# Attention and two MoE layers on one core: the final addition steps through its columns in another order

## The chip, the cores and the metric

The kernel runs on one core of a Trainium2 chip. The metric is the device time of one execution, in microseconds (us). An execution is one launch: all inputs come from HBM and the result goes back to HBM. TensorE (PE) does matrix products and writes them to the accumulation memory PSUM; VectorE (DVE), ScalarE (ACT) and GpSimd (POOL) work on SBUF, the first two also on PSUM; SyncE (SP) issues transfers. Each engine works through its own instructions in program order and waits for others by semaphores.

## The reference

```python
# q, k, v: (4 batches, 8 heads, 576 tokens, 64), float32
q_d = q.reshape(B, H, Sd, factor, D).mean(axis=3)        # factor 4, Sd = 144; k_d, v_d alike
out_d = sm_attn(q_d, k_d, v_d)                           # softmax attention over 144 pooled tokens
out_up = np.repeat(out_d, factor, axis=2)                # each pooled row serves four tokens
mask = np.abs(pos[:, None] - pos[None, :]) < factor      # local attention: 7 neighbours
...
return (out_up + out_local).astype(np.float32)
# x: the sum, as (2304 tokens, 512)
g = h * (1.0 / (1.0 + np.exp(-h)))                       # layer 1: x @ w_in, then @ w_out (d_ff 2048)
g = np.where(h > 0.0, h, alpha * (np.exp(np.minimum(h, 0.0)) - 1.0))   # layer 2, the same shapes
```

The line that matters here is `out_up + out_local`: token t gets the local output of its own and the pooled output of token group t // 4.

## The kernel before, in words

The attention is cut into 16 units: 4 batches by 4 pairs of heads (`attend(i, due)`). Channels lie on the 128 partitions (two heads of 64), tokens lie along the columns. A unit goes through these steps, each a `Job` with an engine, a modelled duration and its predecessors:

- rows of q and k are loaded and turned by TensorE (L742), copied out of PSUM by ScalarE or VectorE (L770, L775), and pooled by fours on VectorE (tile `qkD`); v is pooled by TensorE for the first batch (L815) and by VectorE or GpSimd for the others (tiles `natv` or `lent` to `vd`);
- the local scores (L879) and the pooled scores (L955) go through their softmax: on VectorE the mask, the maxima and sums (tile `small`), on ScalarE the exponentials (L930, L974), on GpSimd mostly the two passes that subtract the maximum or multiply by the inverse sum (tile `ring`);
- TensorE turns the results (L1002, L1025); they are copied to SBUF (L1010, L1036); TensorE forms the pooled output (L1049, 144 columns, copied at L1057 to the tile `own` or `spare`, which the code calls `haD`) and the local output (L1114, in two PSUM banks of 288 columns);
- the join (L1131) adds both: it reads the local output from a PSUM bank `b`, the pooled output from `haD`, and writes the sum to the activations x in SBUF: `xa` (tokens 0 to 1151), `xb` (1152 to 1535) or `tail` (1536 to 2303). The bank becomes free when its join is done.

A unit has three joins of 288 columns: one with 128 partitions and two with 64 (the second bank holds its two heads swapped). In the third batch the cut at token 1536 splits the two 64-partition ones into 96 and 192 columns. There are 56 joins in all, with 40 x 288 + 8 x 192 + 8 x 96 = 13,824 columns.

Behind the joins, x is split into an upper part (`xh`, ScalarE, L1186) and a rest (`xl`, GpSimd or VectorE) and multiplied with the weights of layer 1 on TensorE (L1247 and, after the activation, L1290). These products run between the attention's. From about 238 us on everything is products (L1999, L2102, L1939, L2104, L1941). TensorE's short products at L447 and L460 fill gaps in the first 60 us; they compute nothing that is used.

The order of the work is made by a list scheduler while the program is built: it takes jobs when they are ready by modelled clocks of the engines and puts them out, so each engine's order is fixed in the program. The model's cost of a join depends on its number of columns alone. All work of VectorE and GpSimd passes through a recording helper and therefore stands at line 35 in the profile; tiles tell it apart.

Two other reads of VectorE step through memory, and the prediction uses them. The decoding of weights takes every second 32-bit word of `ws`:

```python
return st.rearrange("p (n w) -> p n w", w=2)     # L511
nc.vector.scalar_tensor_tensor(out(), st[:, :, 0], 13, out(), op0=ALU.logical_shift_right, op1=ALU.bitwise_or)   # L533
```

and the pooling of v sums four rows that lie 64 words apart:

```python
vn = hv.tile[j].rearrange("p (a r d) -> p a d r", a=2, r=FAC)     # L838
```

Of the kernel before, what the change touches and what calls it, by code (L numbers as in the profile page):

```python
# [53 lines left out]
def attention_moe_moe2_kernel(ctx, tc, q, k, v, wi1, wo1, wi2, wo2, out):  # L54
# [5 lines left out]
    P = 128  # L60
    FAC = 4
# [55 lines left out]
    HALF = S // 2  # L117
# [43 lines left out]
    def x_cuts(t0, n):  # L161

        at = sorted({t0, t0 + n} | {a for a, _, _ in X_AT if t0 < a < t0 + n})
        return [(a, e - a) for a, e in zip(at, at[1:])]

    def x_cols(c, t0, n, p0=0, p1=P):
        a, e, x = next(x for x in X_AT if x[0] <= t0 < x[1])
        assert t0 + n <= e
        return x[p0:p1, c, t0 - a:t0 - a + n]
# [500 lines left out]
    def attend(i, due):  # L670

        b, pr = pairs[i]
# [11 lines left out]
        haT, haD = Hold(SAT0 if early else SAT), Hold(SAD0 if early else SAD)  # L684
# [46 lines left out]
        for n_, cells in enumerate(([(0, c) for c in range(NTB - 1)], [(1, c) for c in range(NTB - 1)], [(0, NTB - 1), (1, NTB - 1)])):  # L731
            bank = Hold(banks, "a")
# [19 lines left out]
            o = 0  # L752
            for which in range(2):
                n = TB * sum(w == which for w, _ in cells)
                if n:
                    c0, nc_ = min(c for w, c in cells if w == which), n // TB
# [102 lines left out]
        for part, (s0, s1, halves_, outs) in enumerate(parts):  # L859
# [137 lines left out]
            for g0, g1_ in groups:  # L997
                bank = Hold(banks, "a")
# [16 lines left out]
            for a0_, a1_ in ((0, 2), (2, 3)):  # L1015
                bank = Hold(banks, "a")
# [49 lines left out]
            if b < QUAD_FROM:  # L1066
                for t in outs:
                    bank = Hold(banks, "a")

                    def out_l(t=t, bank=bank):  # L1070
                        vw = hw.tile.rearrange("p (n d) -> p n d", d=D)
                        for w in range(t * NW // 2, (t + 1) * NW // 2):
                            n = a0[w + 1] - a0[w]
                            c0 = (w % 2) * WIN + a0[w] - q0[w]
                            o = a0[w] - t * HALF
                            for j in range(2):
                                nc.tensor.matmul(
                                    bank.tile[j * D:(j + 1) * D, o:o + n],
                                    vw[j * WIN:(j + 1) * WIN, w, :],
                                    aT()[j * WIN:(j + 1) * WIN, w // 2, c0:c0 + n],  # L1080
                                    start=True, stop=True,
                                )

                    def join(t=t, bank=bank):
                        g0 = b * S + t * HALF
                        u0 = t * HALF // FAC
                        nc.vector.tensor_tensor(
                            x_cols(pr, g0, HALF).rearrange("p (m r) -> p m r", r=FAC),
                            bank.tile[:, :HALF].rearrange("p (m r) -> p m r", r=FAC),
                            haD.tile[:, u0:u0 + HALF // FAC].rearrange("p (m o) -> p m o", o=1).to_broadcast([P, HALF // FAC, FAC]),  # L1090
                            op=ALU.add,
                        )

                    pj = Job("P", 0.6, out_l, [lw] + [flips[g] for g in sorted(flips) if t == 1 or g == 0], lat=0.2, takes=[bank], uses=[hw, haT], mode="q")
                    end_ = due[t] if isinstance(due, tuple) else due + 0.5 * t
                    final.append(Job("V", 0.47, join, [pj, ups] + (sum(first_users.values(), []) if b == 1 else second_users if b else []), due=end_, uses=[bank, haD]))
                    x_written[pr, 2 * b + t] = final[-1]
                    if early:
                        first_users[pr].append(final[-1])
                continue  # L1100
# [21 lines left out]
            for t, p0, p1 in ((0, 0, P), (1, 0, D), (1, D, P)):  # L1122
                bank = banko[t]
                g0 = b * S + t * HALF
                for c0, n0 in x_cuts(g0, HALF):
                    c1 = c0 + n0

                    def join(t=t, bank=bank, p0=p0, p1=p1, g0=g0, c0=c0, c1=c1):
                        i0 = (p0 + t * D) % P
                        u0, n_ = (c0 - b * S) // FAC, (c1 - c0) // FAC  # L1130
                        nc.vector.tensor_tensor(  # L1131
                            x_cols(pr, c0, c1 - c0, p0, p1).rearrange("p (m r) -> p m r", r=FAC),
                            bank.tile[i0:i0 + p1 - p0, c0 - g0:c1 - g0].rearrange("p (m r) -> p m r", r=FAC),
                            haD.tile[p0:p1, u0:u0 + n_].rearrange("p (m o) -> p m o", o=1).to_broadcast([p1 - p0, n_, FAC]),
                            op=ALU.add,
                        )

                    end_ = due[t] if isinstance(due, tuple) else due + 0.5 * t
                    job = Job(
                        "V", 0.16 + 0.00106 * (c1 - c0), join,  # L1140
                        [pj, ups] + (sum(first_users.values(), []) if b == 1 else second_users if b else []), due=end_, uses=[bank, haD],
                    )
                    if p0 or c0 > g0:
                        job.after([x_written[pr, 2 * b + t]])
                    final.append(job)
                    x_written[pr, 2 * b + t] = job
                    if early:
                        first_users[pr].append(job)
# [977 lines left out]
    with tc.manual_schedule():  # L2126
# [17 lines left out]
        for i in range(len(pairs)):  # L2144
            b_, pr = pairs[i]
# [110 lines left out]
```

## Time and profile before

| | |
|---|---|
| median of 3 runs | 852.47 us (851.71 to 852.82) |
| profiled execution, its own time | 852.25 us |
| its span, first to last instruction | 850.5 us |
| TensorE, busy | 842.7 us (99%) |
| VectorE, busy | 670.5 us (79%) |
| ScalarE, busy | 559.6 us (66%) |
| GpSimd, busy | 200.3 us (24%) |

Busy shares are averages over stages: up to about 217 us attention and layer 1 run beside each other and all engines take part; after it TensorE has products back to back. TensorE's busy time is modelled from pipelined products and also covers the filling products. The time of the profiled execution is 1.75 us longer than its span, for what lies around the instructions.

### The profile page before, as it was taken

Reading aid. Unit: us, or ns where it says so; the run is one execution under the profiler, and the core shown is the slowest. Engines: PE = TensorE matmul, PEld = TensorE weight load, DVE = VectorE, ACT = ScalarE, POOL = GpSimd, SP = SyncE. Lnnn points to the kernel's source line nnn. Section 1 sums busy time; section 2 is a strip of 40 time slices with the busy share of each in tenths; the row PEclk is TensorE's granted clock in tenths of the full one; section 3 lists DMA queues with packets and bytes.
Section 4 is the critical chain, followed back from the end, with each engine's and each line's share of the span. In section 5 each row is a group of like instructions: output and inputs, shape, how many; then the busy total and the mean of one; then the engine's idle time right before and its main releaser. Section 6 shows DMA issues by size and latency. Waiting matters only on the chain.

```text
span 850.5 us, 17258 instructions
## 1 busy us (share of the span) xinstructions
PE 842.7 (99%) x6507; PEld 780.8 (92%) x6507; DVE 670.5 (79%) x1348; ACT 559.6 (66%) x1270; POOL 200.3 (24%) x229
## 2 busy tenths in 40 slices
PE   8999999999999999999999999999999999999998
PEld 6778787778899999999999998899998999999998
DVE  6777776665889998958969789479889999487497
ACT  5778764455479886455398596377499884473672
POOL 7677785574200100000000121000020102002012
DMA  9888785331346354043287475163686670561612
GB/s 167 195 186 184 163 260 121 91 92 59 124 127 195 122 173 126 1 150 106 70 258 266 175 240 198 75 223 106 214 277 214 216 270 5 208 201 38 220 42 75
DMA packets 120483, 132.59 MB, mean 156 GB/s; under 512 B 65040, under 2 KB 97040, under 8 KB 120272
## 3 DMA queue, kind: packets, MB, share of 16 engines
q1 hardware_dynamic: 118032, 130.90, 50.7%
q8 instruction: 51, 0.84, 0.4%
q10 hardware_dynamic: 2368, 0.59, 0.4%
q14 instruction: 32, 0.26, 0.1%
HBM read 89.26 MB, written 42.21 MB: 155 GB/s over the span
## 4 chain that ended last, share of the span: by engine, by line
PE 96%; DVE 1%; POOL 1%; ACT 1%; DMA 0%; issue 0%; SPq 0%; POOLq 0%; ACTq 0%; DVEq 0%
PE b L1999 34%; PE b L1941 14%; PE b L2102 8%; PE b L1290 8%; PE b L2104 8%; PE b L1247 8%; PE b L1939 7%; PE b L742 2%; PE b L1114 1%; PE b L879 1%; PE b L1002 1%; PE b L1025 1%; PE b L1049 1%; PE b L955 1%; PE b L815 1%; PE b L447 0%
## 5 line engine op out<-in xcount | busy, mean ns | idle before, releaser
L1999 PE MATMUL b<-xhr,xaw 128*128 128x384 f32 x288 | 77.3, 335 | 0.0
L1290 PE MATMUL b<-gx,w 128*128 128x512 f32 x288 | 75.3, 399 | 0.0
L1999 PE MATMUL b<-xhr,w 128*128 128x384 f32 x256 | 66.8, 335 | 0.0
L1247 PE MATMUL b<-xh,w 128*128 128x512 f32 (+1 forms) x176 | 62.9, 394 | 1.0 <-POOL w L35 0.6
L1290 PEld LDWEIGHTS b<-gx,w 128*128 128x128 f32 x288 | 52.1, 188 | 11.0 <-issue 1.0
L2011 ACT COPY hg<-b 128x384 f32<-128x384 f32 x60 | 29.0, 483 | 45.5 <-PE b L1999 45.2
L35 DVE TENSOR_TENSOR part<-b,part 128x256 f32<-128x256 f32 (+3 forms) x94 | 43.1, 506 | 17.5 <-PE b L1941 16.1
L35 DVE TENSOR_TENSOR b<-b,hg 128x384 f32<-128x384 f32 x60 | 33.6, 561 | 27.9 <-PE b L1999 20.4
L35 POOL TENSOR_TENSOR ring<-ring,small 128x640 f32<-128x640 f32 (+1 forms) x41 | 47.7, 1170 | 29.5 <-DVE small L35 29.2
L1999 PE MATMUL b<-xlr,xaw 128*128 128x384 f32 x160 | 53.5, 334 | 0.0
L1999 PEld LDWEIGHTS b<-xhr,xaw 128*128 128x128 f32 x288 | 52.4, 188 | 0.0
L35 DVE TENSOR_TENSOR xlr<-tail,xhr 128x768 fp32r<-128x768 f32 x42 | 39.9, 954 | 14.3 <-ACT xhr L1416 13.9
L1941 PE MATMUL b<-w,gx 128*128 128x256 f32 x264 | 49.8, 283 | 0.0
L2102 PE MATMUL b<-grw,w 128*128 128x384 f32 x192 | 49.7, 334 | 0.0
L2102 PE MATMUL b<-gx,w 128*128 128x384 f32 x192 | 49.3, 334 | 0.0
L2104 PE MATMUL b<-w,gx 128*128 128x512 f32 x156 | 46.9, 389 | 0.0
L1999 PEld LDWEIGHTS b<-xhr,w 128*128 128x128 f32 x256 | 46.4, 188 | 0.2
L1999 PE MATMUL b<-xlr,w 128*128 128x384 f32 x128 | 42.8, 334 | 0.0
L35 POOL TENSOR_TENSOR gx<-hg,grw 128x384 fp32r<-128x384 f32 x4 | 4.4, 1108 | 160.5 <-ACT grw L1416 160.5
L1416 ACT CAST xhr<-tail 128x768 fp32r<-128x768 f32 x42 | 35.7, 850 | 9.4 <-DVE tail L35 9.3
L2104 PE MATMUL b<-w,grw 128*128 128x512 f32 x132 | 41.6, 389 | 0.0
L1247 PEld LDWEIGHTS b<-xh,w 128*128 128x128 f32 x176 | 32.4, 188 | 8.5 <-POOL w L35 1.0
(352 smaller groups left out, 2616.8 us busy)
## 6 DMA issues: line engine op xcount, KB each, us to landing
ws<-in_moe_w_in_dram SPq DMA_DIRECT2D x30, 512.0 KB
ws<-in_moe_w_out_dram SPq DMA_DIRECT2D x30, 512.0 KB
tailr<-xs SPq DMA_DIRECT2D x28, 384.0 KB
xs<-xhr SPq DMA_DIRECT2D x21, 384.0 KB
xs<-xlr SPq DMA_DIRECT2D x21, 384.0 KB
x<-part SPq DMA_DIRECT2D x6, 768.0 KB
tail<-x SPq DMA_DIRECT2D x12, 384.0 KB
vw<-in_v_dram SPq DMA_DIRECT2D x28, 144.0 KB
```

The source lines that it names most:

```text
L35: ins = x(*args, **rest)
L742: nc.tensor.transpose(bank.tile[:, n * TB:(n + 1) * TB], row(which, c)[:TB], ident[:TB, :TB])
L815: nc.tensor.matmul(bankv[j].tile[:HS, c * D:(c + 1) * D], pooler()[rows_, n, :], vw[rows_, w, :], start=n == 0, stop=n == len(POOLED_BY) - ...
L1247: nc.tensor.matmul(ph.tile[:, o:o + m_], w[a][:, c, :], x, start=c == 0 and m == 0, stop=c == KC - 1 and m == 2, skip_group_check=True,)
L1290: nc.tensor.matmul(y[d].tile[:, :W], wo[m // 2][:, d * P:(d + 1) * P], gg(m % 2, 0, W), start=f == 0 and m == 0, stop=fin and m == 2)
L1416: a = Job("A", ACT_[width], lambda: nc.scalar.copy(hi(), at()), preds, gate)
L1939: nc.tensor.matmul(y, wm[:, sl], gm, start=first, stop=last_, skip_group_check=True)
L1941: nc.tensor.matmul(y, gm[:, sl], wm, start=first, stop=last_, skip_group_check=True)
L1999: nc.tensor.matmul(acc_, a[:, cs], b[:, c, :], start=fresh and c == 0 and m == 0, stop=c == 1 and m == 2, skip_group_check=True,)
L2011: snap[after, j] = [Job("A", ACT_[NB], lambda dst=dst, acc_=acc_: nc.scalar.copy(dst, acc_), [], gate, due=soon)]
L2102: nc.tensor.matmul(y[d][:, :NB], wm[:, sl], gm, start=first, stop=last_)
L2104: nc.tensor.matmul(y[d], gm[:, sl], wm, start=first, stop=last_)
```

## The change

Only the form of the join's access patterns changes. Before, the walk over a join's columns was in the order in which they lie in memory: pooled column m outside, its four tokens r inside. Now r is outside and m inside: the walk reads columns 0, 4, 8, ... of the PSUM bank and writes them to columns 0, 4, 8, ... of x, then columns 1, 5, 9, ..., and so on. The pooled operand, which was read four times in place for each column, is now read through in order, four times over. The values added and the places written are the same.

```diff
                         nc.vector.tensor_tensor(
-                            x_cols(pr, c0, c1 - c0, p0, p1).rearrange("p (m r) -> p m r", r=FAC),
-                            bank.tile[i0:i0 + p1 - p0, c0 - g0:c1 - g0].rearrange("p (m r) -> p m r", r=FAC),
-                            haD.tile[p0:p1, u0:u0 + n_].rearrange("p (m o) -> p m o", o=1).to_broadcast([p1 - p0, n_, FAC]),
+                            x_cols(pr, c0, c1 - c0, p0, p1).rearrange("p (m r) -> p r m", r=FAC),
+                            bank.tile[i0:i0 + p1 - p0, c0 - g0:c1 - g0].rearrange("p (m r) -> p r m", r=FAC),
+                            haD.tile[p0:p1, u0:u0 + n_].rearrange("p (o m) -> p o m", o=1).to_broadcast([p1 - p0, FAC, n_]),
                             op=ALU.add,
                         )
```

The same edit stands in a second join (L1087) behind `if b < QUAD_FROM`; QUAD_FROM is 0, so that branch is not built. No instruction moves on any engine. On VectorE 56 rows change their shape. The first piece is VectorE's order in the first unit (at about 21 us of the profile); `b_98` and `b_99` are PSUM banks, `own` is the pooled output, `small` holds maxima and sums:

```order
 L35 COPY xa<-b_93 128x480
-L35 TENSOR_TENSOR xa<-b_98,own 128x288
-L35 TENSOR_REDUCE small<-small 128x3
-L35 RECIPROCAL small<-small 128x3
-L35 TENSOR_TENSOR xa<-b_99,own 64x288
+L35 TENSOR_TENSOR xa<-b_98,own 128x4x72
+L35 TENSOR_REDUCE small<-small 128x3
+L35 RECIPROCAL small<-small 128x3
+L35 TENSOR_TENSOR xa<-b_99,own 64x4x72
 L35 TENSOR_REDUCE small<-b_96 128x5
```

The two joins stand at the same places; a contiguous run of 288 columns has become 4 rows of 72. The second piece is VectorE's order in the first unit of the third batch (at about 127 us), where the joins stand between the steps of another unit's softmax:

```order
-L35 TENSOR_TENSOR xb<-b_94,own 128x288
-L35 TENSOR_TENSOR tail<-b_96,own 64x192
-L35 TENSOR_REDUCE small<-ring_118 128x10
-L35 TENSOR_REDUCE small<-small 128x10
-L35 RECIPROCAL small<-small 128x10
-L35 TENSOR_TENSOR xb<-b_96,own 64x96
+L35 TENSOR_TENSOR xb<-b_94,own 128x4x72
+L35 TENSOR_TENSOR tail<-b_96,own 64x4x48
+L35 TENSOR_REDUCE small<-ring_118 128x10
+L35 TENSOR_REDUCE small<-small 128x10
+L35 RECIPROCAL small<-small 128x10
+L35 TENSOR_TENSOR xb<-b_96,own 64x4x24
```

Here too only the shapes differ: the sums of `ring` and their inverse stay behind three joins.

## Rows read from the trace of the kernel before

**Rows 1.** The page's busy times: engine, busy us (share of the span), instructions.
```profile
PE 842.7 (99%) x6507; PEld 780.8 (92%) x6507; DVE 670.5 (79%) x1348; ACT 559.6 (66%) x1270; POOL 200.3 (24%) x229
```

**Rows 2.** The table of stretches: busy us of each engine, clock, DMA, GB/s.
```profile
21.30:34.20 12.90, 12.45 (x285) 9.74 (x277) 12.17 (x33) 8.94 (x29) 9.01 (x10) 1.00 0.92 248
...
58.00:126.00 68.00, 67.96 (x799) 54.95 (x798) 50.69 (x103) 49.03 (x127) 53.16 (x54) 1.00 0.82 197
126.00:217.00 91.00, 90.64 (x1032) 71.34 (x1029) 55.23 (x127) 46.17 (x134) 51.50 (x58) 1.00 0.34 88
217.00:850.50 633.50, 630.44 (x3817) 614.18 (x3815) 522.71 (x1016) 425.88 (x900) 54.23 (x49) 1.00 0.47 158
```

**Rows 3.** Groups on VectorE: output, inputs, shapes, count | busy us, mean ns | idle.
```profile
L35 DVE TENSOR_TENSOR xa<-b,own 64x288 f32<-64x288 f32 x12 | 5.5, 454 | 3.6 <-PE b L1114 3.2
...
L35 DVE TENSOR_TENSOR tail<-b,own 64x192 f32<-64x192 f32 x8 | 2.8, 352 | 0.2
...
L35 DVE TENSOR_TENSOR xb<-b,own 64x96 f32<-64x96 f32 x8 | 2.0, 255 | 5.2 <-PE b L1114 2.5 <-ACT own L1057 2.5
```

**Rows 4.** The same view: contiguous reads, and reads that step.
```profile
L35 DVE SCALAR_TENSOR_TENSOR raw<-ws,raw 128x512 int32<-128x512 int32 x48 | 33.1, 691 | 5.2 <-ACT raw L529 5.1
...
L35 DVE TENSOR_REDUCE qkD<-qk 128x144 f32<-128x576 f32 x20 | 14.0, 742 | 0.1
...
L35 DVE TENSOR_TENSOR part<-b,part 128x512 f32<-128x512 f32 x12 | 7.5, 682 | 7.9 <-PE b L1941 7.9
L35 DVE TENSOR_REDUCE vd<-natv 72x128 f32<-72x512 f32 x7 | 7.5, 1066 | 0.0
```

**Rows 5.** The chain that ended last, 18 to 60 us: start, us, what.
```profile
21.34 0.46 DVE xa L35
...
42.08 0.46 DVE xa L35
...
42.56 0.03 ACT xh L1186
...
42.88 0.26 ACT qk L770
```

**Rows 6.** Waits of TensorE's weight loads, 20 to 36 us: us, times, longest.
```profile
PEld b L815 <- DVE xa L35: 0.4, 1, 0.4
```

**Rows 7.** Timeline of VectorE, 38 to 43 us: start, us, what, idle before.
```profile
38.75 1.43 DVE L35 TENSOR_TENSOR xa<-b,own 64x288 f32<-64x288 f32 x3
41.10 1.43 DVE L35 TENSOR_TENSOR xa<-b,spare 64x288 f32<-64x288 f32 x3 [0.92 <-ACT xh L1186]
```

**Rows 8.** Timeline of all engines, 126 to 131 us.
```profile
126.85 0.73 DVE L35 TENSOR_TENSOR xb<-b,own 64x96 f32<-64x96 f32 x2
...
127.61 0.36 DVE L35 TENSOR_TENSOR tail<-b,own 64x192 f32<-64x192 f32 x1
...
129.30 2.13 POOL L35 TENSOR_TENSOR ring<-ring,small 128x640 f32<-128x640 f32 x2 [3.37 <-DVE small L35]
...
130.62 0.31 PEld L1002 LDWEIGHTS b<-own,ring 128*128 128x128 f32 x3 [0.43 <-POOL ring L35]
```

**Rows 9.** The chain that ended last, 128 to 143 us.
```profile
138.53 0.36 DVE tail L35
...
138.93 1.66 PE b L1247 x6
```

**Rows 10.** Timeline of all engines, 178 to 184 us.
```profile
178.35 1.43 DVE L35 TENSOR_TENSOR tail<-b,own 64x288 f32<-64x288 f32 x3
...
181.24 2.13 POOL L35 TENSOR_TENSOR ring<-ring,small 128x640 f32<-128x640 f32 x2 [1.59 <-DVE small L35]
...
183.41 0.40 PEld L1025 LDWEIGHTS b<-own,ring 112*72 112x72 f32 x4 [0.40 <-POOL ring L35]
```

**Rows 11.** Timeline of VectorE behind two other triples, at 72.86 and 163.36 us.
```profile
75.92 0.42 DVE L35 SCALAR_TENSOR_TENSOR t<-t,b 128x256 f32<-128x256 f32 x1 [0.91 <-ACT t L1269]
...
165.63 0.89 DVE L35 SCALAR_TENSOR_TENSOR ring<-b,mask 128x320 f32<-128x320 f32 x2 [0.60 <-PE b L879]
```

More of the change, by code (lines that the diff above doesn't have):

```diff
@@ L1087, in join @@
                         nc.vector.tensor_tensor(
-                            x_cols(pr, g0, HALF).rearrange("p (m r) -> p m r", r=FAC),
-                            bank.tile[:, :HALF].rearrange("p (m r) -> p m r", r=FAC),
-                            haD.tile[:, u0:u0 + HALF // FAC].rearrange("p (m o) -> p m o", o=1).to_broadcast([P, HALF // FAC, FAC]),
+                            x_cols(pr, g0, HALF).rearrange("p (m r) -> p r m", r=FAC),
+                            bank.tile[:, :HALF].rearrange("p (m r) -> p r m", r=FAC),
+                            haD.tile[:, u0:u0 + HALF // FAC].rearrange("p (o m) -> p o m", o=1).to_broadcast([P, FAC, HALF // FAC]),
                             op=ALU.add,
```

## The prediction, as it was put on record

> **What bounds the kernel now.** I read the page's busy times first. TensorE has 842.7 us of a span of 850.5 us; VectorE, where the change sits, has 670.5 us, or 79% [rows 1]. A longer VectorE operation costs time only where TensorE comes to wait for it. So I read the table of stretches next: from 217 us on TensorE is busy for 630.4 of 633.5 us and no join is left there, so the joins, which run from 21 to 217 us, decide by how much that last stretch starts later. Before it, VectorE is busy for 50.7 of 68 us and then 55.2 of 91 us, so it has gaps that can swallow something; but from 21.3 to 34.2 us it is busy for 12.17 of 12.90 us and has none to speak of [rows 2]. TensorE's clock column is 1.00 throughout, its full 2.4 GHz level, so no term comes from the clock. Then I followed each of the 16 units in the timeline, the chain and the list of waits: what follows its joins on VectorE, who waits for that, and how wide the next gap is.
>
> **The operation itself.** Nothing is added, removed or moved; 56 joins change the step of two of their three streams. Before, a join of 288 columns takes 454 ns and one of 96 takes 255 ns [rows 3]. That is (454 - 255) / 192 = 1.04 ns per column and 255 - 96 x 1.04 = 155 ns besides. A contiguous addition of 512 columns takes 682 ns [rows 4], which is 155 + 512 x 1.03. So the join already runs at the full rate, fourfold reading of the pooled column included, and there is nothing to gain per column.
>
> Now the read of PSUM and the write to SBUF both step by 4 words (16 bytes); only the pooled operand becomes contiguous. No row has a step of 4 words. Two rows bracket it. The decoding of weights reads every second word: 691 ns for 512 columns, 1.05 ns per column, no penalty. The pooling of v steps by 64 words: 1066 ns for 512, or (1066 - 155) / 512 = 1.78 ns per column, where the same reduction of contiguous columns takes (742 - 155) / 576 = 1.02 [rows 4]. So a stepping stream costs between nothing and 0.76 ns per column; two of them between nothing and 1.52, if their costs add. With 13,824 columns that is 0 to 21 us of VectorE.
>
> The row at 2 words is free and the row at 64 is not. The Trainium skill, page "SBUF — State Buffer", section "Door 1: The DMA port swizzle", has a note that SBUF is reached in lines of 16 bytes, that two accesses in a row must fall in one line for the full rate, and that PSUM has lines of 8 bytes. The free row agrees (two of its words lie in 16 bytes), and by this note a step of 16 bytes pays on both streams, which speaks against the change. The page "Vector Engine (DVE) Microarchitecture Reference", section "5.2 Measured stream behaviour on trn2 (trn3 not measured)", asks for runs of two adjacent words; by that the 2-word row would have to be slow, and its 691 ns says that it isn't.
>
> Between 0 and 1.52 I take 1.0 ns more per column: the free row still uses every second word that it passes, the join only every fourth, and it does so on two streams at once, so I put it nearer to the row that pays and a little over one stepping stream. A join of 288 then takes 454 + 288 = 742 ns, and VectorE has 13.8 us more.
>
> **Where it lies on the path.** Five places have no cover.
>
> 1. 21.3 to 34.2 us. Six joins stand in VectorE's row of work. The chain of waits runs through the first at 21.34 us [rows 5], and at its end TensorE's L815 waits for the bank of the sixth, with 0.4 us of waiting already [rows 6]. 6 x 288 ns = 1.73 us. Of the stretch's 0.73 us of idle time most is hand-over between neighbours; I let 0.3 us absorb: 1.43 us.
> 2. The fourth unit's three joins at 41.10 us [rows 7]. The chain goes through them: the split `xh` on ScalarE waits for the last (42.08 to 42.54), and behind it in ScalarE's order stands the copy of `qk` (42.88), which leads to the pooled scores [rows 5]. 864 columns: 0.86 us. The third unit's joins at 38.75 us cost nothing: behind them VectorE is idle for 0.92 us, waiting for others [rows 7].
> 3. 126.85 us. Three joins (96, 288 and 192 columns) stand ahead of the sums that GpSimd waits 3.37 us for, and the weights of TensorE's L1002 wait 0.43 us for GpSimd [rows 8]. 576 columns: 0.58 us. The other 288 columns of that unit lie behind those sums and are covered.
> 4. 136.3 to 138.9 us. The chain goes through five joins, the last at 138.53 us, and then to TensorE's L1247 at 138.93, which needs the bank [rows 9]. 864 columns: 0.86 us.
> 5. 178.35 us. Behind the three joins come sums; GpSimd is idle for 1.59 us until they are done, and TensorE's L1025 waits 0.40 us for GpSimd [rows 10]. 0.86 us.
>
> Together 1728 + 864 + 576 + 864 + 864 = 4896 columns of 13,824, or 4.90 us less 0.3 = 4.6 us.
>
> The other 8928 columns I cost at nothing. Their cover is VectorE's next gap: 0.91 us behind the joins at 72.86 us, 0.60 us behind those at 163.36 us, where another 0.26 us stays over [rows 11] and falls on sums that TensorE needs later. With the cover gone they would cost 8.9 us more. What each covered triple makes late is the next unit's mask and sums on VectorE, then GpSimd's passes over `ring`, then L1002 and L1025; TensorE has products of layer 1 to do meanwhile, and its order is fixed. Nothing brings time back: after 217 us TensorE runs without a break.
>
> **The sum.** 852.25 us (the profiled execution's own time, 1.75 us over its span; 0.22 under the median of the runs) + 4.6 = 856.85 us; I say 856.8. With one stepping stream's 0.76 ns it is 852.25 + 3.72 - 0.3 = 855.7. With 1.52 ns it is 852.25 + 7.44 - 0.3, and the joins of 288 grow by 438 ns, so three of them (1.31 us) overrun the gaps of 0.92, 0.91 and 0.60 us by 0.39, 0.40 and 0.71 us: 860.9.
>
> **Rivals.**
>
> - *The step is free* (the other side). If VectorE serves a step of 4 words like that of 2 words (691 ns), the joins stay at 454 ns and the time at 852.3 us. For it: the only small step in the trace costs nothing. Against it: the 64-word row, and that PSUM must be read in steps too, which no row shows. It decides below about 0.4 ns per column, where 4896 columns less 0.3 us fall under 1.7 us. 0.18.
> - *The two streams add.* Read and write each wait on their own and one after the other, so the price is 1.52 ns per column and the covers overrun: 860.9 us. For it: a join has no buffer that a row would show. Against it: a stream that steps alone costs 0.76, and read and write of one instruction can run side by side. 0.16. (The Trainium skill's Microarchitecture Reference, section 5.2, lists an output that steps 24 words at 2.50 ns per column; an estimate from that page, 1.46 more per column, would give about 860.5 us. No row here shows a stepping output.)
> - *Only the first 46 us count.* TensorE has 0.36 us of idle time from 126 to 217 us [rows 2], nearly all at place 4; places 3 and 5 show only waiting weight loads. It may have more in hand than I think; then places 1, 2 and 4 alone give 1.43 + 0.86 + 0.86: 855.4 us, and without place 4 854.5. For it: 0.4 us of waiting by a weight load is not yet TensorE idle. Against it: each load started right when GpSimd was done. 0.17.
>
> **How the numbers follow.** My forecast (prices of 0.76 to 1.25 ns and five places: 855.7 to 858.1 us) gets 0.43. The rest of 0.06 is for more than 861 us, where covers fail that I counted. A measurement of this kernel tells some 0.2%, or 1.7 us, from no change. Faster by that: 0.02, since no join can lose more than some ns. Within it: 0.18, of which 0.16 is the rest of the free step and 0.02 the low end of the third rival. Slower: 0.80, all the rest. The range goes from 852.3, the free step's time, to 861.0, the adding streams'; outside stay the 0.06 above and about half of the free step, 0.15 in all.
>
> **What would show it.** In the profile of the changed kernel: the group of joins 64x288 (now 4 x 72) at about 742 ns, between 454 and 892; VectorE's busy time at 684 us; TensorE's waits for `xa` at L815 and for `tail` at L1247 longer by about 0.3 and 0.9 us; the stretch of unbroken products after 217 us as long as before, but begun 4.6 us later, 2.3 us of it lost by 46 us and the rest between 126 and 184 us. I am wrong if the joins stay at 454 ns, or if they are slower and TensorE starts its last stretch on time; then the covers were wider than the gaps that I read.

## The result and the profile after

The changed kernel takes 856.92 us (median of 5 runs, 855.36 to 857.35) where the kernel before takes 852.36 us (5 runs, 851.48 to 852.82): a ratio of 1.0051, with an interval of 1.0036 to 1.0066. The change costs about 4.6 us; the forecast was 856.8. The profiled execution took 856.92 us, 4.67 us more than the one before (852.25); its span is 855.2 us, 4.7 more.

The page's busy times after (columns as in [rows 1]):

```profile
PE 843.7 (99%) x6507; PEld 780.6 (91%) x6507; DVE 680.3 (80%) x1348; ACT 560.0 (65%) x1270; POOL 203.3 (24%) x229
```

VectorE has 9.8 us more than before. The joins' groups on VectorE, which answer to [rows 3]:

```profile
L35 DVE TENSOR_TENSOR xa<-b,own 64x288 f32<-64x288 f32 x12 | 8.2, 680 | 3.6 <-PE b L1114 3.2
...
L35 DVE TENSOR_TENSOR tail<-b,own 64x192 f32<-64x192 f32 x8 | 4.0, 500 | 0.2
...
L35 DVE TENSOR_TENSOR xb<-b,own 64x96 f32<-64x96 f32 x8 | 2.7, 332 | 5.0 <-ACT own L1057 2.6 <-PE b L1114 2.3
```

A join of 288 columns has grown by 226 ns, or 226 / 288 = 0.785 ns per column; those of 192 and 96 by 148 and 77 ns, 0.77 and 0.80 per column. The cost is per column; the time besides stays about the same, (680 - 332) / 192 = 1.81 ns per column leaving 158 ns, before 155. The table of stretches after, by its own time (the last row begins 4.7 us later than that of [rows 2], as much as the span has grown):

```profile
21.30:34.20 12.90, 12.04 (x291) 9.68 (x280) 12.32 (x33) 8.37 (x26) 8.56 (x10) 1.00 1.09 260
58.00:126.00 68.00, 66.88 (x769) 53.25 (x768) 52.61 (x102) 48.50 (x127) 51.90 (x53) 1.00 0.80 192
126.00:217.00 91.00, 89.49 (x1004) 70.03 (x1001) 59.34 (x127) 45.57 (x133) 53.37 (x59) 1.00 0.36 95
...
221.70:855.20 633.50, 630.42 (x3817) 614.15 (x3815) 522.78 (x1017) 425.77 (x900) 57.17 (x49) 1.00 0.47 158
```

The last 633.5 us hold the same 3817 products with the same busy time (630.42 us, before 630.44): nothing is lost or given back there, and the clock column stays at 1.00. TensorE's idle time has grown in each of the three rows above that one: from 0.45 to 0.86 us between 21.3 and 34.2 us, from 0.04 to 1.12 between 58 and 126, and from 0.36 to 1.51 between 126 and 217. The forecast had nothing between 58 and 126 us.

What TensorE's products wait for in the whole span after (us, times, longest):

```profile
PE b L955 <- DVE qkD L35: 1.2, 1, 1.2
...
PE b L1247 <- DVE tail L35: 1.0, 1, 1.0
PE b L1025 <- DVE yo L35: 0.8, 1, 0.8
PE b L1002 <- POOL ring L35: 0.7, 3, 0.4
...
PE b L1247 <- DVE xa L35: 0.5, 1, 0.5
PE b L1247 <- DVE t L35: 0.4, 1, 0.4
```

Before, this list had 1.0 for `qkD`, 0.3 for `tail`, 0.4 for `yo` and 0.2 for GpSimd's `ring`, and neither the wait for `xa` nor that for `t` at L1247.

Since no instruction moves on any engine, each product of TensorE can be paired with the same one before, and the difference of the two start times shows where time is lost. The table gives how much the lag grows, in us, at the place where it grows (time of before; medians over the products between two places). "Start" is the difference already there behind the first loads, at about 14 us; it differs by over a microsecond from run to run and has nothing to do with joins. The other columns are runs of the next section: the stepping order in one batch of four only, and a copy ahead of each join of before.

| place, us | after | only batch 0 | only batch 1 | only batch 2 | only batch 3 | copy ahead |
|---|---|---|---|---|---|---|
| start | 0.17 | -0.07 | -1.27 | -1.00 | 0.02 | -1.30 |
| 24.5 (L1025) | 0.42 | 0.42 | 0.31* | 0.38* | 0.31* | 1.10* |
| 34 (L815) | 0.00 | 0.00 | 0.05 | 0.05 | 0.05 | 0.05 |
| 42.5 (L879) and 45.9 (L955) | 0.72 | 0.70 | 0.01 | 0.00 | 0.00 | 0.62 |
| 59.9 (L1247) | 0.50 | -0.02 | 0.46 | -0.02 | 0.02 | 0.33 |
| 68.6 (L1049) | 0.15 | 0.03 | 0.21 | 0.03 | 0.01 | 0.14 |
| 95.6 (L1247) | 0.39 | 0.00 | 0.39 | 0.03 | 0.02 | 0.27 |
| 119.6 (L1002) | 0.41 | 0.00 | 0.46 | 0.00 | 0.00 | 0.26 |
| 130.6 (L1002) | 0.36 | 0.00 | 0.01 | 0.35 | 0.00 | 0.45 |
| 138.9 (L1247) | 0.61 | -0.02 | 0.02 | 0.65 | -0.03 | 0.68 |
| 165.3 (L955) | 0.17 | 0.00 | 0.00 | 0.13 | 0.00 | 0.11 |
| 179.9 (L1247) and 183.4 (L1025) | 0.78 | 0.02 | 0.01 | 0.00 | 0.76 | 0.55 |
| all | 4.68 | 1.07 | 0.66 | 0.59 | 1.18 | 3.24 |

The fields with * hold a difference of 0.3 us or more at about 28 us (L815) that also comes up in a run whose joins are as short as before (0.27 us, the read in steps below), so in the runs of batches 1 to 3 it isn't the joins' doing. The 1.10 of the last column are 0.29 at 24.5 us and 0.81 at 28, more than in any other run; TensorE's load at L815 sits idle there for 0.7 us, and the profile names no releaser. What causes this is open.

### The profile page after: what moved, and what is told of

The parts are those of the page before. It is cut to its first block, busy times and chain, and to the rows that moved or that the text cites. A ratio compares the mean times of both kernels' runs of the same rounds, so it can differ in the third digit from the quotient of the medians.

```text
span 855.2 us, 17258 instructions
## 1 busy us (share of the span) xinstructions
PE 843.7 (99%) x6507; PEld 780.6 (91%) x6507; DVE 680.3 (80%) x1348; ACT 560.0 (65%) x1270; POOL 203.3 (24%) x229
## 4 chain that ended last, share of the span: by engine, by line
PE 90%; DVE 4%; POOL 2%; issue 1%; DMA 1%; ACT 1%; SPq 0%; POOLq 0%; ACTq 0%; DVEq 0%
PE b L1999 34%; PE b L1941 14%; PE b L2102 8%; PE b L2104 8%; PE b L1939 7%; PE b L1290 6%; PE b L1247 5%; POOL ring L35 1%; PE b L742 1%; PE b L1114 1%; PE b L1002 1%; DMA nat<-in_q_dram 1%; DVE small L35 1%; PE b L1049 1%; PE b L1025 1%
## 5 line engine op out<-in xcount | busy, mean ns | idle before, releaser
L1999 PE MATMUL b<-xhr,xaw 128*128 128x384 f32 x288 | 77.3, 335 | 0.0
L1999 PE MATMUL b<-xhr,w 128*128 128x384 f32 x256 | 66.9, 335 | 0.0
L1247 PE MATMUL b<-xh,w 128*128 128x512 f32 (+1 forms) x176 | 63.0, 395 | 2.5 <-DVE tail L35 1.0
L1999 PE MATMUL b<-xlr,xaw 128*128 128x384 f32 x160 | 53.5, 334 | 0.0
L1999 PEld LDWEIGHTS b<-xhr,xaw 128*128 128x128 f32 x288 | 52.4, 188 | 0.0
L1999 PEld LDWEIGHTS b<-xhr,w 128*128 128x128 f32 x256 | 46.4, 188 | 0.2
L1999 PE MATMUL b<-xlr,w 128*128 128x384 f32 x128 | 42.8, 334 | 0.0
L1247 PEld LDWEIGHTS b<-xh,w 128*128 128x128 f32 x176 | 32.4, 188 | 10.3 <-DVE tail L35 1.4
```

The lines of the kernel that those rows point to most:

```text
L1247: nc.tensor.matmul(ph.tile[:, o:o + m_], w[a][:, c, :], x, start=c == 0 and m == 0, stop=c == KC - 1 and m == 2, skip_group_check=True,)
L1999: nc.tensor.matmul(acc_, a[:, cs], b[:, c, :], start=fresh and c == 0 and m == 0, stop=c == 1 and m == 2, skip_group_check=True,)
```

## The experiments

Two questions were open. Which of the two stepping streams pays, and from which step on? And does VectorE's longer time alone explain the 4.6 us, at places that the forecast did not have? Edits are given against the changed kernel's join unless they say otherwise.

### Which stream pays

One stream at a time. First the bank is read in steps of 4 and x is written in order; then the other way round.

```diff
-  x_cols(...).rearrange("p (m r) -> p r m", r=FAC),           # first run: the write
+  x_cols(...).rearrange("p (r m) -> p r m", r=FAC),
-  bank.tile[...].rearrange("p (m r) -> p r m", r=FAC),        # second run: the read
+  bank.tile[...].rearrange("p (r m) -> p r m", r=FAC),
```

> The 56 joins read PSUM in steps of 4 words as in the change, but write x contiguously, so the tokens inside each join's columns land in another order (the output is not the reference's). The changed kernel's join of 64x288 took 680 ns, 0.78 ns per column over the 454 ns of before. Theory A (a stream that steps sets the rate, and two that step run side by side): about 680 ns here too, TensorE's first L1999 about 4.5 us later than before. Theory B (both streams pay, and the prices add): about 567 ns. Theory C (only the write to SBUF pays): 454 ns and the time of before.

> The mirror image: the joins read PSUM contiguously and write x in steps of 4 words; the tokens inside each join's columns land in another order (the output is not the reference's). Theory A (the slowest stream sets the rate): about 680 ns. Theory B (prices add): about 567 ns, and with the read-only run's excess it makes up 226 ns. Theory C (only the write pays): 680 ns here and 454 ns in the read-only run; its opposite (only the read pays): 454 ns here.

The first join group with the read in steps, then with the write in steps:

```profile
L35 DVE TENSOR_TENSOR xa<-b,own 64x288 f32<-64x288 f32 x12 | 5.5, 455 | 3.6 <-PE b L1114 3.2
```

```profile
L35 DVE TENSOR_TENSOR xa<-b,own 64x288 f32<-64x288 f32 x12 | 8.2, 684 | 3.6 <-PE b L1114 3.2
```

The read of PSUM in steps of 4 words is free (455 ns; 850.92 us), and the write to SBUF pays all of it (684 ns; 857.08 us, the time of the change). Both are single runs, with 852.57 us for the kernel before beside them; their times scatter by a microsecond, and the join's own duration decides. The second run loses its time at the same places as the change: its lag grows by 4.57 us behind the start, against 4.51.

### From which step on

Steps of 2 (write and read), and pairs of neighbours with a hop of 4:

```diff
-  ....rearrange("p (m r) -> p r m", r=FAC)
+  ....rearrange("p (m a s) -> p s m a", a=2, s=2)             # step 2; pairs: "p (m s a) -> p s m a"
-  haD....rearrange("p (o m) -> p o m", o=1).to_broadcast([p1 - p0, FAC, n_])
+  haD....rearrange("p (o m q) -> p o m q", o=1, q=1).to_broadcast([p1 - p0, 2, n_, 2])
```

> The same result as the reference's, but the walk goes over every second column (2 x 144 columns, step of 2 words on the read and on the write). If the decoding of weights, which steps by 2 words and takes 691 ns for 512 columns, tells the rule for PSUM and for writes too: 454 to 460 ns for 64x288 and 852 to 853 us. If any step at all costs what a step of 4 words costs: 680 ns and some 4.5 us more. A value between, some 567 ns, if PSUM pays from 2 words on and SBUF doesn't and prices add.

> The same result as the reference's; the walk takes two neighbouring columns, then hops over two (2 x 72 x 2). If a step costs because each access leaves the place of the last one, a pair halves the number of such accesses: about 567 ns for 64x288. If two neighbours at a time are enough for the full rate: 454 to 460 ns and the time of before. If a row of the pattern costs something when it ends (144 rows of 2 here, 4 rows of 72 in the change), more than 680 ns.

Both give 456 ns for `xa` 64x288 and times of 851.6 and 852.2 us: no price. Then two steps that are no power of two, 24 and 3 words on both streams:

```diff
-  ....rearrange("p (m r) -> p r m", r=FAC)
+  ....rearrange("p (m r) -> p r m", r=24)                     # and r=3
-  haD.tile[p0:p1, u0:u0 + n_]...to_broadcast([p1 - p0, FAC, n_])
+  haD.tile[p0:p1, u0:u0 + n_ // 6]...to_broadcast([p1 - p0, 24, n_ // 6])   # step 24
+  haD.tile[p0:p1, :(c1 - c0) // 3]...to_broadcast([p1 - p0, 3, (c1 - c0) // 3])   # step 3
```

> The walk steps by 24 words on the read and on the write (24 x 12 columns); the pooled operand is read contiguously and is the wrong one for most columns, so the output is not the reference's. If the price of a stepping write does not depend on the step: 64x288 at about 680 ns and 228.3 us from L815 to L1999. If it is higher for 24 words (2.50 ns per column in place of 1.82): 155 + 288 x 2.5 = 875 ns, and the loss grows more than in proportion, as more covers overrun: over 232 us.

> Both the read of PSUM and the write to SBUF step by 3 words (in three passes), and the pooled operand is read through in order as 96 (or 64, 32) columns from the start of its tile, so the sum takes other pooled columns than the reference's. Earlier runs gave 456 ns for a join of 288 columns that steps by 2 words and 676 to 688 ns for one that writes in steps of 4, the read in steps being free. Theory G (the write pays by 16-byte pieces of SBUF that it touches one after the other): with 3 words between neighbours a piece takes two of them in one case of four, so three pieces per four columns, each at the 1.82 ns of a step of 4: 1.37 ns per column, about 550 ns. The same with fixed pairs of columns: one pair in three shares a piece, 454 + 2/3 x 226 = about 605 ns. Rival (any step over 2 words pays the full price): 680 ns. Rival (a step that is no power of two spreads over the memory and is free): 455 ns. The time follows: 852.4 us at 455, about 854 to 855.5 at 550 to 605, 857 at 680.

The groups with a step of 24, then with a step of 3:

```profile
L35 DVE TENSOR_TENSOR xa<-b,own 64x288 f32<-64x288 f32 x12 | 9.6, 799 | 3.5 <-PE b L1114 3.2
...
L35 DVE TENSOR_TENSOR tail<-b,own 64x192 f32<-64x192 f32 x8 | 5.0, 622 | 0.2
...
L35 DVE TENSOR_TENSOR xb<-b,own 64x96 f32<-64x96 f32 x8 | 2.6, 327 | 4.9 <-ACT own L1057 2.6 <-PE b L1114 2.2
```

```profile
L35 DVE TENSOR_TENSOR xa<-b,own 64x288 f32<-64x288 f32 x12 | 6.6, 551 | 3.6 <-PE b L1114 3.2
...
L35 DVE TENSOR_TENSOR tail<-b,own 64x192 f32<-64x192 f32 x8 | 3.3, 414 | 0.2
...
L35 DVE TENSOR_TENSOR xb<-b,own 64x96 f32<-64x96 f32 x8 | 2.3, 289 | 5.1 <-ACT own L1057 2.5 <-PE b L1114 2.5
```

At step 3 the expectation of 550 ns for pieces of 16 bytes is met (551). Pieces of 4 words, each at 1.82 ns when the next column lies in another one, and three pieces touched per four columns, give 155 + 192 x 1.37 = 418 ns and 155 + 96 x 1.37 = 287 ns for the smaller joins; measured are 414 and 289. Fixed pairs (605 ns), the full price (680) and a free step (455) are out. One rival was not tried apart: a price of 1.82 / 4 = 0.455 ns for each word that the walk passes, with the full rate as its floor, gives the same times at 2, 3 and 4 words and for the pairs. The whole execution took 853.69 us (a single run).

At step 24 the price depends on how many columns a pass has: with 4 columns per pass (96 in all) 327 ns, the same as with a step of 4; with 8 and 12 columns 622 and 799 ns, that is (622 - 155) / 192 = 2.43 and (799 - 155) / 288 = 2.24 ns per column. So 16-byte pieces are not the whole rule: a large step can cost more than one of 4 words; nor is the price one per word passed, which would give 24 x 0.455 = 10.9 ns per column here. What sets the further price was not tried, nor which of the two streams pays it, nor any step between 4 and 24 words. This kernel took 861.1 us.

### Where the time is lost

The stepping order in one batch only, four runs:

```diff
-  ....rearrange("p (m r) -> p r m", r=FAC)
+  ....rearrange("p (m r) -> p r m" if b == k else "p (m r) -> p m r", r=FAC)   # stepping in batch k alone; haD alike
```

> Only the 12 joins of the first batch (21 to 43 us) step; the others stay as before. Measure: the distance from TensorE's first L815 to its first L1999, 223.8 us before and 228.3 after. Theory P (as predicted, places 1 and 2 at the measured 0.785 ns per column): 1.06 + 0.68, so 225.5 us. Theory Q (what the changed kernel's trace shows: 0.4 us by 24.5 us, nothing at the L815 that I named, 0.7 us at 42 to 46 us): 224.9 us. Nothing lost after 46 us in either.

> Only the 12 joins of the second batch (58.9 to 106 us) step. Theory P (as predicted, all covered by VectorE's gaps): distance from L815 to L1999 as before, 223.8 us. Theory Q (four losses that I had not counted: 0.48 us at L1247 near 60 us, which needs the bank, 0.19, 0.39 and 0.41 us near 69, 96 and 120 us): 225.2 to 225.3 us.

> Only the 20 joins of the third batch (127 to 165 us) step. Theory P (places 3 and 4 at 0.785 ns per column): 0.45 + 0.68, so 224.9 us from L815 to L1999. Theory Q (0.35 near 131 us, 0.66 near 139, 0.26 near 165): 225.1 us. The two differ by 0.2 us here; what tells them apart is whether a loss stands near 165 us, and whether the first is smaller than 0.45 us.

> Only the 12 joins of the fourth batch (178 to 217 us) step. Theory P (place 5 alone, 0.68 us, all of it at L1025 near 183 us): 224.5 us from L815 to L1999. Theory Q (0.4 us at L742 and L1247 near 180 us, which need the banks of the joins, 0.13 us at L1025): 224.3 us. If the last joins at 216 us delayed the products after 237 us, more than 224.5.

The times are single runs (853.32, 852.9, 852.83 and 853.44 us; before beside them 853.33) and, with the scatter of the start, cannot tell a microsecond. By the measure named beforehand, the distance from L815 to L1999 (before 223.8 us, after the change 228.3), the four have 224.9, 225.8, 225.4 and 225.0 us: the first as theory Q has it, the others 0.3 to 0.7 us above it, mostly because this distance also holds the 0.3 to 0.4 us at 28 us that aren't the joins' doing. The lags in the table above tell them apart: at its own places batch 0 costs 0.42 + 0.70 = 1.12 us, batch 1 1.52, batch 2 1.13 and batch 3 0.76 us. These are the places of the full change, and they add up to 4.53 us where the full change has 4.68 - 0.17 = 4.51. So the loss is a sum of independent places, none of them given back later, and the largest share comes from batch 1, for which the forecast had nothing. In the fourth batch theory P had all of the loss at L1025; 0.54 us of it stand near 180 us, at L742 and L1247, where theory Q had 0.4.

### VectorE's time alone

The joins of before, with a contiguous copy of a quarter of the columns from the same bank ahead of each, into a tile that nobody reads:

```diff
+  nc.vector.tensor_copy(scratch[p0:p1, :(c1 - c0) // 4], bank.tile[i0:i0 + p1 - p0, c0 - g0:c0 - g0 + (c1 - c0) // 4])
   nc.vector.tensor_tensor(...)                                # the join of before
```

> The joins are contiguous as before; ahead of each, VectorE copies a quarter of the join's columns (72, 48 or 24) from the same PSUM bank to a scratch tile, contiguously, which nothing reads. That lengthens VectorE's work at the same 56 places by some 0.23 us each (155 ns and 1.04 ns per column, from the joins of before), nearly what the stepping write adds (0.226 us for 288 columns), without any step. If only VectorE's time counts: the distance from L815 to L1999 grows by 4.4 to 5.2 us, with the losses at the same instructions (L1247 near 60 and 139 us, L1002 near 131). If the stepping write also hindered other engines at SBUF: less than 3.5 us here.

The groups of copy and join, and VectorE's timeline of one unit:

```profile
L35 DVE CAST scratch<-b 64x72 bf16<-64x72 f32 x24 | 5.5, 231 | 4.8 <-PE b L1114 4.1
L35 DVE TENSOR_TENSOR xa<-b,own 64x288 f32<-64x288 f32 x12 | 5.4, 451 | 0.1
```

```profile
59.39 0.23 DVE L35 CAST scratch<-b 64x72 bf16<-64x72 f32 x1 [0.67 <-PE b L1114]
59.55 0.45 DVE L35 TENSOR_TENSOR xa<-b,own 64x288 f32<-64x288 f32 x1
...
60.90 0.45 DVE L35 TENSOR_TENSOR xa<-b,own 64x288 f32<-64x288 f32 x1
```

A copy lasts 231 ns, but the join starts 0.16 us after it, so copy and join overlap a little: the unit's three joins take 59.39 to 61.35, 1.96 us, where they took 1.43 before and take 2.11 stepping. That is 0.53 us more instead of 0.68, or 78%. The places from 42.5 us on add up to 3.41 us of lag (last column of the table) against the change's 4.09, or 83%, and they are the same places. The kernel took 855.89 us (median of 4, 854.89 to 856.43; before beside it 852.03), a ratio of 1.0043 with an interval of 1.0028 to 1.0058. The distance from L815 to L1999 grew by 4.5 us (to 228.4), as expected, but 0.81 of it is the difference at 28 us whose cause is open; the comparison of places leaves it out. So it is the time on VectorE that costs, about in proportion; something that stepping writes do to other engines isn't needed to explain it.

### A scheduler that knows the price

The changed kernel, with the measured cost of a join in the scheduler's model, so that it orders the work anew:

```diff
-  "V", 0.16 + 0.00106 * (c1 - c0), join,
+  "V", 0.16 + 0.00185 * (c1 - c0), join,
```

> The changed kernel, and the scheduler's modelled cost of a join raised from 0.16 + 0.00106 to 0.16 + 0.00185 us per column, as measured, so that the order of all jobs is planned anew. If the loss stands where the fixed order leaves no room for longer joins, a plan that knows of them wins part of the 4.5 us back: 853.5 to 856 us. If other waits come with the new order (the due times in the kernel were set for the old one): 857 us or more.

856.98 us (median of 4, 856.17 to 858.08), a ratio of 1.0061 with an interval of 1.0044 to 1.0078: the median is that of the change, nothing comes back. Two rows of its table of stretches:

```profile
58.00:126.00 68.00, 65.32 (x674) 51.42 (x665) 47.45 (x96) 45.39 (x116) 53.23 (x54) 1.00 0.77 190
126.00:217.00 91.00, 90.74 (x1045) 71.02 (x1044) 57.52 (x122) 49.34 (x144) 56.63 (x63) 1.00 0.36 95
```

TensorE's idle time from 126 to 217 us falls from 1.51 to 0.26 us, but from 58 to 126 us it rises from 1.12 to 2.68. What the new order saves in the second stretch it loses in the first. From 21 to 58 us it saves another 1.4 us (2.96 to 1.56), and the profiled execution, at 856.17 us the shortest of the four, is 0.75 us below the changed kernel's; the other three range up to 858.08, so no gain is shown. Whether another order would recover the time is left open.

## Why the forecast was right, and where its parts were not

**The total is right because two errors cancel, and that is luck.** The direction, the mechanism (longer joins that TensorE comes to wait for, nothing regained after 217 us) and the time (856.8 forecast, 856.9 measured) hold. The price per column was too high and the number of columns on the path too low: 1.0 ns x 4896 columns less 0.3 us was forecast; measured is 0.785 ns, and 4.51 / 0.785 = some 5750 columns. Where the time goes differs more: 2.3 us were forecast by 46 us and 2.3 between 126 and 184; measured are 1.14 by 46 us, 1.45 between 58 and 126, and 1.92 from there on.

**The price.** The step that failed is "I put it nearer to the row that pays and a little over one stepping stream". It is one stepping stream, as the pooling of v in [rows 4] shows it for a read (0.76 against 0.785), because the read of PSUM in steps costs nothing. That a write at 4 words and a read at 64 cost the same may be chance: at 24 words the price was higher than at 4. The Trainium skill, page "SBUF — State Buffer", section "Door 1: The DMA port swizzle", asks for two accesses in a 16-byte line of SBUF, and the steps of 2, 3 and 4 words at 456, 551 and 684 ns agree. It ties its 8-byte lines of PSUM to slower matmuls; the forecast carried them over to a VectorE read at 16 bytes, and the 455 ns say that this read doesn't pay. The rival of adding streams (1.52 ns per column) falls with that free read, and the free step (454 ns) by the join's 680.

**Place 1 (forecast 1.43 us, at the measured price 1.06; measured 0.42).** The forecast read [rows 6] as TensorE waiting for the bank of the sixth join. After the change the same load and VectorE's work around it stand like this (start, duration, idle before and its releaser):

```profile
34.20 0.41 DVE L35 COPY ring<-b 128x256 f32<-128x256 f32 x1
...
34.64 0.67 DVE L35 TENSOR_TENSOR xa<-b,spare 64x288 f32<-64x288 f32 x1
...
34.84 1.18 PEld L815 LDWEIGHTS b<-yo,natv 57*72 57x72 f32 x34 [0.36 <-DVE ring L35]
```

The join runs until 35.31 us, and the load starts at 34.84: it didn't wait for the join, and its idle time of 0.36 us is what it was before. The forecast had TensorE's wait for `xa` at L815 grow by about 0.3 us; it isn't there. The releaser in [rows 6] was only the last VectorE operation that ended ahead of the load, by 0.06 us. Of the six joins two, ahead of L1025 at 24.5 us, seem to be on the path: 2 x 226 = 452 ns, measured 0.42 us, and the wait of L1025 for `yo` has gone from 0.4 to 0.8 us. The split into these two and the other four was read from the trace and not tried by itself.

**Places 2 to 4** hold, at the measured price; place 5 holds in its size, but not in most of its way. Place 2: 864 x 0.785 = 0.68 us, measured 0.72. Place 3: 0.45, measured 0.36. Place 4: 0.68, measured 0.61, with the wait of L1247 for `tail` that was forecast (0.3 us before, 1.0 after). Place 5: 0.68, measured 0.78, but the forecast had all of it at L1025, through GpSimd. Two weight loads of the changed kernel, near 180 us in the time of before:

```profile
183.69 0.45 PEld L742 LDWEIGHTS b<-own,spare 96*128 96x128 f32 x5 [0.43 <-DVE tail L35]
...
184.41 0.19 PEld L1247 LDWEIGHTS b<-xh,w 128*128 128x128 f32 x1 [0.26 <-DVE tail L35]
```

They start 0.05 us behind the ends of the second and the third join (183.64 and 184.35 us), and behind them the lag has grown by 0.55 us; only 0.12 is added at L1025. Before, they started 0.11 and 0.18 us behind those ends (179.30 and 179.78), and no list of waits named the joins. So the joins reach TensorE first through these banks, a link that the forecast did not have. The rival that only the first 46 us count is out: place 3 cost 0.36 us, and by the load of place 5 another 0.67 was lost.

**The places costed at nothing** gave 1.62 us: 1.45 in batch 1 (59.9, 68.6, 95.6 and 119.6 us) and 0.17 at 165.3 us. The step that failed is "The other 8928 columns I cost at nothing". Rows of the kernel before, VectorE and TensorE at 59 us, show the first of them:

```profile
58.93 1.43 DVE L35 TENSOR_TENSOR xa<-b,own 64x288 f32<-64x288 f32 x3 [0.66 <-PE b L1114]
```

```profile
59.23 0.67 PE L955 MATMUL b<-qkD 64*64 64x144 f32 x12
...
59.93 0.19 PEld L1247 LDWEIGHTS b<-xh,w 128*128 128x128 f32 x1 [0.29 <-DVE xa L35]
59.93 0.50 PE L1247 MATMUL b<-xh,w 128*128 128x512 f32 x1
```

L1247 writes to the bank that the second join frees; in the trace that join ends at 59.88 us, and the load starts 0.05 us later. TensorE had products until 59.90 and went on at 59.93, so the list of its products' waits does not name this join. The list of its weight loads does, with 0.3 us, and it names `t` for the L1247 at 95.6 us with 0.2. The forecast took such waits of weight loads as places 1, 3 and 5 and left these two out. After the change, the timeline there reads:

```profile
60.24 2.11 DVE L35 TENSOR_TENSOR xa<-b,own 64x288 f32<-64x288 f32 x3 [0.67 <-PE b L1114]
...
61.71 0.50 PE L1247 MATMUL b<-xh,w 128*128 128x512 f32 x1 [0.49 <-DVE xa L35]
```

The second join ends at 61.65 us and L1247's load again follows 0.05 us behind: 0.49 us of waiting for two joins that have grown by 0.45 us. In the same way the waits at L1247 for `t` (95.6 us) and at L1002 for GpSimd's `ring` (119.6 us) are links that VectorE's gaps did not cover: the forecast had read the width of the gap on VectorE, not the slack of the engine that waits at its far end. Which of the joins at 90.10 and 104.53 us each of these two goes back to was not tried by itself; the run of batch 1 alone shows that they are that batch's.

**Covers that held.** The triple at 72.86 us with 0.91 us behind it [rows 11] shows no lag between 69 and 95 us. That at 163.36 us had 0.60 us for 3 x 226 = 678 ns; 0.08 us should stay over, and 0.17 were lost (0.13 with batch 2 alone).

**The share that is lost rises with the price.** Per ns that a join of 288 grows, TensorE loses more: 97 ns (step 3) cost 1.47 us behind the start, 226 ns cost 4.51 and 345 ns (step 24) 8.64, or 15, 20 and 25 ns for each ns. The gaps swallow a smaller part of a large growth than of a small one, so a price scaled linearly from one size misleads for another.

## What to carry to other kernels

Put the steps of an access pattern on the side of VectorE's operation where they are free: here a read of PSUM in steps of 4 words cost nothing, while a write to SBUF in the same steps cost 75% more per column; steps of 2 words, or pairs of neighbours, cost nothing on either. To price a longer operation on an engine that is not the bound, go through every load and product of the bound engine that starts close behind an end of that operation, whether or not a list of waits names it. Here loads 0.05, 0.11 and 0.18 us behind a join's end (59.93, 179.41 and 179.96 us) lost time, and one at 0.06 (34.25 us) lost none, because it did not wait for that join. So nearness and a named wait only point at a place; whether the load needs what the operation frees decides. A list scheduler that is told the right cost need not find a better order.

## What the runs showed of the hardware

- VectorE's addition with a PSUM read in steps of 4 words runs at the full rate: 455 ns for 288 columns, against 454 contiguous.
- A VectorE write to SBUF takes 456 ns at a step of 2 words, 551 at 3 and 684 at 4 for 288 columns, as 16-byte pieces would make it (2 and 3 with both streams stepping). At 24 words it depends on the length of a pass as well: 1.79, 2.43 and 2.24 ns per column for 4, 8 and 12 columns a pass (both streams stepping).
- The Trainium skill, page "Vector Engine (DVE) Microarchitecture Reference", section "5.2 Measured stream behaviour on trn2 (trn3 not measured)", gives the full rate only to runs of two adjacent words; the join at a step of 2 words (456 ns) runs at it without any two adjacent. Its 2.50 ns for an output at 24 words is near the 2.43 of the join of 192 columns here, less near the 2.24 of 288, and not the 1.79 of 96.
